# Softmax attention beside a gated MLP on one core: the order of P.V and output groups at the end, two instead of three units normalised on VectorE, and leads of TensorE's row matmuls by stretch

## The chip, the core and the metric

The kernel runs on one core of one Trainium2 chip. A core has five engines that run their own instruction streams in order and meet through semaphores: TensorE (PE; its weight loads are shown as PEld), VectorE (DVE), ScalarE (ACT), GpSimd (POOL) and SyncE (SP), which here issues all DMA transfers. TensorE writes its results into eight PSUM banks of 128 x 512 f32. The metric is device microseconds of one execution.

## What is computed

```python
def reference(A_x, A_wqkv, A_wo, B_x, B_w1, B_w3, B_w2):
    x = A_x                                   # 1 x 2048 x 512, bf16
    xn = _layernorm(x, axis=-1)
    return x + _A_ref(xn, A_wqkv, A_wo) + _B_ref(xn, B_w1, B_w3, B_w2)

def _A_ref(x, wqkv, wo):                      # 32 heads of 16
    ...
    scores = jnp.einsum("bhqd,bhkd->bhqk", q, k) * (Dh ** -0.5)
    p = _softmax(scores, axis=-1)
    o = jnp.einsum("bhqk,bhkd->bhqd", p, v)
    return o.transpose(0, 2, 1, 3).reshape(B, S, D) @ wo

def _B_ref(x, w1, w3, w2):                    # F = 1792
    h = _silu(x @ w1) * (x @ w3)
    return h @ w2
```

The layer norm has no parameters. The scores, 32 heads x 2048 x 2048, are far the largest part: each is computed twice here, once for the row maximum and once for the exponential.

## The kernel before, in words

**Units.** The work of the attention is cut into 81 units, numbered 0 to 80: four heads (a group g, eight of them) by 256 queries, or by 128 queries at the start and in the last eight groups. The last group's four units are 77 to 80. Each unit goes through these steps:

1. *Row matmuls and maxima.* TensorE computes scores with the queries on the partitions, two matmuls of 512 keys for two heads into two banks (line 1047, "P1" in the code, banks 0 and 1 or 2 and 3 by turns). VectorE reduces the 128 x 1024 scores to 128 x 2 partial maxima (line 1089). There are 1024 such pairs of matmuls and 1024 such reductions. A pair waits for the reduction before the last, which frees its banks.
2. *Final maximum.* Partial maxima become a negated row maximum, on VectorE in the first and last units (L1226), on GpSimd in the others. It is split into two bf16 numbers in Z (L1174, L1176).
3. *Opening of a unit.* The two rows of Z are put beside the queries in QT, so that the second score matmul subtracts the maximum by itself. Near the start and in the last units a TensorE tile does this (identity matmuls on QT and Z, in the helper at L593) and ScalarE evacuates it into QT (L808).
4. *Scores again and exponential.* TensorE computes scores with the keys on the partitions (L1313, a score group fills one of banks 4 to 7, after the last maximum any bank), ScalarE takes the exponential into PT, one bank at a time (L1326) or two at once (L1356). A unit of 128 queries has 16 such groups.
5. *P.V.* TensorE multiplies PT by V, which has a column of ones for the sum (L579, 16 key tiles of four matmuls each).
6. *Normalisation.* Ordinary way: ScalarE evacuates to U (L1421), SP moves the sums to Lc (L1442), GpSimd inverts them (L1446), SP writes them to DRAM and reads them back spread over the partitions (L1451, L1455), GpSimd multiplies into `onorm` (L1466; the buffers wk_on and on_b). Fast way, for the last NFPV units (`FAST_PV`): TensorE repeats the sum over 32 rows with matmuls on `ones_t`, VectorE inverts (L1411) and multiplies (L1413) straight from PSUM.

**Other work.** TensorE also runs projections, the MLP (its evacuations at L849, L851, L855), and output tiles. The last four output tiles, 12 to 15, are cut in two: an earlier part with x and the MLP, kept in SBUF, and OUTB, eight matmuls of `onorm` by `wo` (`wo,wk_on` at L593). The eighth needs group 7, that is unit 77 for tile 12 and so on to unit 80 for tile 15. VectorE adds the two parts into osb (L960) and SP stores them (L899).

**What sets the order.** All engines' streams are written out before the kernel runs, by a planner inside `_build` that follows each engine's free time with a cost for each operation and picks the next one. For TensorE `pick_pe` chooses between the next pair for a maximum (`p1_cand`), the next score group (`p2_cand`) and other matmuls (`col_cand`, or a filling matmul on xnT and ident from `fill_cand`). Other matmuls run as long as the row matmuls are not due: pairs for a maximum are due `A_LEAD` us before VectorE runs out of work, score groups `ROW_LEAD` before ScalarE does (`RELAX` later when the units behind are not ready). `COUPLE` lets a row matmul start with the one before; `KEEP` holds score groups off the rows that the next pair needs; `PAIR_WAIT` and `COVER` decide when ScalarE takes two banks at once; `URG_WAIT`, `HORIZON` and `LOAD_RATE` decide when TensorE is filled up; `MATE` prefers neighbouring banks; `PV_LEFT` tells when a unit's P.V may take a bank. These stand in `K`. In `p1_cand`, after every 32nd pair:

```python
p1_n[0] += 1
if p1_n[0] % STRETCH == 0:
    K.at(LEADS.get(p1_n[0] // STRETCH, {}))
```

`K.at` puts all values back to their base and then sets those of the stretch's entry. Entry n is read after pair 32 n, so entry 0 is never read. `LEADS` is empty in the kernel before.

In `col_cand` the active tiles are looked at in a fixed rank, and the one whose next matmul can start first is taken:

```python
st = P.pe_start(t.mode, None, P.ready("pe", reads, writes))
if best is None or st < best[0] - 1e-6:
    best = (st, t, reads, writes, g[2])
```

`red_n` counts the maxima that were put out, `NP1` is 1024; at `red_n[0] >= NP1` the last maximum is done.

## Time and profile before

| | |
|---|---|
| median of 3 runs | 1198.83 us (1197.3 to 1199.32) |
| the profiled execution | 1196.87 us, of which the span from first to last instruction is 1195.2 |
| TensorE, busy | 1122.1 us (94%) |
| VectorE, busy | 1178.8 us (99%) |
| ScalarE, busy | 1171.8 us (98%) |
| GpSimd, busy | 466.5 us (39%) |
| first maximum starts, last opening of a unit | 14.75 us, 1178.73 us |
| granted TensorE clock, mean | 0.999 |

How to read it: a busy time is the union of an engine's instructions. The mean of one instruction in a group is its own length; where instructions overlap in a pipeline (exponentials have a mean of 643 ns), a row of several in the timeline gives the pitch, its length divided by the count. In timelines the columns are start and length in us, engine, line, operation, output and input, the count that was merged, and in brackets the idle time ahead and what ended it. In a table by stretches of time each engine has its busy time and, in brackets, its instructions; the last three columns are the granted clock, the share of the DMA engines and GB/s.

### The profile page before, as it was taken

The page shows a single profiled execution, that of the slowest core. Times are in us where ns is not written, and L with a number is a line of the kernel's source. Part 1 is how long each engine was busy: PE and PEld are TensorE (multiplying, and loading weights), DVE is VectorE, ACT ScalarE, POOL GpSimd, SP SyncE. Part 2 cuts the span into 40 slices and gives each one's busy share as a digit, 9 for nine tenths or more (in the row PEclk, how much of TensorE's full clock was granted, in tenths as well). Part 3 has the DMA queues.
Part 4 walks back from the last instruction along what each step waited for, and adds up shares of the span by engine and source line. Part 5 has one row for each costly group of instructions (what it writes and reads, how often), then busy time and mean ns, then how long its engine had stood idle before and what let it go on. Part 6 is the DMA issues. An engine that isn't in the chain of part 4 may idle for free.

```text
span 1195.2 us, 34930 instructions
## 1 busy us (share of the span) xinstructions
PE 1122.1 (94%) x14546; PEld 495.0 (41%) x14711; DVE 1178.8 (99%) x1082; ACT 1171.8 (98%) x2324; POOL 466.5 (39%) x940
## 2 busy tenths in 40 slices
PE   8999999999999999999999999999989999899998
PEld 3433333343333343333443333333333555555454
DVE  8999999999999999999999999999999999999995
ACT  7899999999999999999999999999999999999997
POOL 7253645324654323656234345522133333324220
PEclk9999999999999999999999999999999999999999
DMA  6422222012212101221011121010000111000000
GB/s 194 116 51 77 59 66 68 15 40 61 52 33 60 40 19 37 57 51 42 26 37 41 48 55 44 25 28 20 22 16 19 46 33 27 20 16 16 10 12 22
DMA packets 131978, 51.54 MB, mean 43 GB/s; under 512 B 99940, under 2 KB 131820, under 8 KB 131820
## 3 DMA queue, kind: packets, MB, share of 16 engines
q1 hardware_dynamic: 131820, 49.31, 16.6%
q8 instruction: 115, 1.88, 0.7%
q14 instruction: 43, 0.35, 0.1%
HBM read 38.86 MB, written 6.74 MB: 38 GB/s over the span
## 4 chain that ended last, share of the span: by engine, by line
ACT 47%; PE 36%; DVE 14%; issue 2%; DMA 0%; POOL 0%; SPq 0%; POOLq 0%
ACT PT L1326 35%; DVE part L1089 13%; PE ps L593 12%; PE ps L1313 11%; PE ps L579 8%; ACT PT L1356 5%; PE ps L1047 5%; ACT th L849 2%; ACT zg L851 1%; ACT U L1421 1%; ACT ub L855 1%; ACT kq L755 1%; DMA PT<-in_A_x_dram 0%; PE ps L677 0%; ACT QT L808 0%
## 5 line engine op out<-in xcount | busy, mean ns | idle before, releaser
L1089 DVE TENSOR_REDUCE part<-ps 128x2 f32<-128x1024 f32 x1024 | 1160.1, 1210 | 0.8 <-PE ps L1047 0.7
L1326 ACT ACTIVATE PT<-ps 128x512 bf16<-128x512 f32 x1826 | 958.8, 643 | 2.1 <-PE ps L1313 0.9
L1313 PE MATMUL ps<-QT,KT 32*128 32x256 bf16 (+1 forms) x5184 | 564.9, 249 | 10.1 <-ACT PT L1356 5.8
L1047 PE MATMUL ps<-KT,QT 32*128 32x512 bf16 x2048 | 400.0, 384 | 5.7 <-DVE part L1089 2.1
L1313 PEld LDWEIGHTS ps<-QT,KT 32*128 32x128 bf16 x5184 | 234.0, 92 | 235.8 <-issue 96.9
L1446 POOL TENSOR_TENSOR Rc<-Lc,mone 128x8 f32<-128x8 f32 (+1 forms) x78 | 109.0, 1397 | 202.5 <-DMA Lc<-U 202.3
L579 PE MATMUL ps<-PT,Vaug 128*17 128x256 bf16 (+1 forms) x5184 | 180.5, 252 | 4.5 <-ACT zg L851 1.5
L593 PE MATMUL ps<-xnT,ident 128*128 128x512 bf16 (+1 forms) x540 | 158.4, 345 | 20.3 <-ACT PT L1356 4.6
L593 PE MATMUL ps<-xnT,w 128*128 128x512 bf16 (+1 forms) x553 | 145.9, 330 | 13.8 <-ACT zg L851 5.3
L1047 PEld LDWEIGHTS ps<-KT,QT 32*128 32x128 bf16 x2048 | 97.9, 91 | 114.3 <-issue 51.5
L579 PEld LDWEIGHTS ps<-PT,Vaug 128*17 128x17 bf16 x5184 | 90.6, 89 | 79.2 <-issue 56.1
L1356 ACT ACTIVATE PT<-ps 128x1024 bf16<-128x1024 f32 x111 | 114.8, 1062 | 1.2 <-PE ps L1313 1.0
L1197 POOL TENSOR_TENSOR mx<-part 128x16 f32<-128x16 f32 (+1 forms) x70 | 14.6, 208 | 223.0 <-DVE part L1089 222.9
L836 POOL TENSOR_TENSOR a<-zg,ub 128x512 f32<-128x512 bf16 x56 | 64.5, 1152 | 68.4 <-ACT ub L855 68.4
L593 PEld LDWEIGHTS ps<-xnT,ident 128*128 128x128 bf16 x617 | 46.5, 96 | 86.5 <-ACT PT L1326 43.4
L593 PEld LDWEIGHTS ps<-xnT,w 128*128 128x128 bf16 x588 | 44.8, 97 | 83.4 <-issue 49.0
L593 PE MATMUL ps<-w,PT 128*128 128x512 bf16 (+1 forms) x268 | 70.1, 332 | 3.3 <-ACT U L1421 1.6
L838 POOL TENSOR_TENSOR PT<-a,t 128x512 bf16<-128x512 f32 x56 | 70.9, 1266 | 2.9
L1466 POOL TENSOR_TENSOR wk_on<-U,R 128x128 bf16<-128x128 f32 (+1 forms) x45 | 24.8, 551 | 66.3 <-DMA R<-rd 66.3
L1466 POOL TENSOR_TENSOR on_b<-U,R 128x256 bf16<-128x256 f32 (+1 forms) x33 | 23.4, 709 | 51.9 <-DMA R<-rd 51.7
L851 ACT ACTIVATE zg<-ps 128x512 bf16<-128x512 f32 x56 | 37.3, 667 | 0.0
L855 ACT ACTIVATE ub<-ps 128x512 bf16<-128x512 f32 x56 | 37.2, 664 | 0.0
(90 smaller groups left out, 552.6 us busy)
## 6 DMA issues: line engine op xcount, KB each, us to landing
w<-in_B_w_dram SPq DMA_DIRECT2D x112, 128.0 KB
R<-rd SPq DMA_DIRECT2D x47, 128.0 KB
QT<-qd SPq DMA_DIRECT2D x31, 128.0 KB
KT<-kd SPq DMA_DIRECT2D x28, 128.0 KB
xr<-in_A_x_dram SPq DMA_DIRECT2D x16, 128.0 KB
out_dram<-osb SPq DMA_DIRECT2D x16, 128.0 KB
R<-rd SPq DMA_DIRECT2D x31, 64.0 KB
qd<-kq SPq DMA_DIRECT2D x15, 128.0 KB
```

The lines of the kernel that those rows point to most:

```text
L579: ins = e.matmul(bank(bk)[32 * i:32 * i + m, c0 + a:c0 + b], make_lhsT(i), rhs if (a, b) == (0, ncols) else rhs[:, a:b], start=start, stop ...
L593: return e.matmul(bank(bk)[0:rows, c0 + a:c0 + b], lhsT, rhs if (a, b) == (0, ncols) else rhs[:, a:b], start=start, stop=stop, **kw)
L836: q.append(_Item(lambda e: e.tensor_tensor(a32[:, :], zg[:, ss, :], ub[:, ss, :], ALU.mult), [("zg", ss), ("ub", ss)], [("a32",)], 1.1, 1.25))
L838: q.append(_Item(lambda e: e.tensor_tensor(hT[:, hslot(idx), :], a32[:, :], t1[:, :], ALU.mult), [("a32",), ("t1",)], [("hT", hslot(idx))] ...
L851: _Item(lambda e: e.activation(zg[:, ss, :], bank(bk), ACTF.Identity, scale=0.5), [("ps", bk)], [("zg", ss)], _c_act(512), cb=part_done, n ...
L855: return [_Item(lambda e: e.activation(ub[:, ss, :], bank(bk), ACTF.Identity), [("ps", bk)], [("ub", ss)], _c_act(512), cb=part_done)]
L1047: ins = e.matmul(bank(2 * sl + i), QT[32 * j:32 * j + 32, qs, q * 128:(q + 1) * 128], KT[32 * j:32 * j + 32, g, c_ * 512:(c_ + 1) * 512], ...
L1089: redq.append(_Item(lambda e: e.tensor_reduce(dst, pair_ap.rearrange("p (a b) -> p a b", b=512), AX.X, ALU.max), writes, [("part", par, qt ...
L1313: ins = e.matmul(bank(b)[:, i * nq:(i + 1) * nq], KT[32 * j:32 * j + 32, g, (k0 + i) * 128:(k0 + i + 1) * 128], QT[32 * j:32 * j + 32, qs, ...
L1326: expq.append(_Item(lambda e: e.activation(PT[:, sl, :], bank(b), ACTF.Exp, scale=SCALE), [("ps", b)], [pt_key(sl)], _c_act(512), cb=cb, e ...
L1356: return _Item(lambda e: e.activation(PT[:, s0:s1 + 1:s1 - s0, :], ps8[:, b0:b1 + 1:b1 - b0, :], ACTF.Exp, scale=SCALE), [("ps", b0), ("ps ...
L1446: poolq["nrm"].append(_Item(lambda e: e.tensor_tensor(Rc[:, pp, 0:nl], Lc[:, pp, 0:nl], mone[:, 0:nl], ALU.pow), [("Lc", pp), ("mone",)], ...
```

## The change

Three things: a term in the choice between the active tiles, the number of units that are normalised the fast way, and a table of leads.

```diff
-    LEADS = {}
+    LEADS = {
+        0: {'PAIR_WAIT': 0.108, 'URG_WAIT': 0.098},
+        1: {'ROW_LEAD': 0.465, 'COUPLE': 0.167, 'A_LEAD': 0.651},
+        2: {'PV_LEFT': 6, 'RELAX': 0.065, 'A_LEAD': 0.649},
...
+        12: {'URG_WAIT': 0.098, 'COVER': 0.917, 'LOAD_RATE': 4870},
+        15: {'MATE': 0.117, 'A_LEAD': 0.571, 'PV_LEFT': 6, 'URG_WAIT': 0.059},
...
+        27: {'PV_LEFT_S': 2, 'ROW_LEAD': 0.43, 'PAIR_WAIT': 0.185, 'LOAD_RATE': 4785},
+        30: {'PAIR_WAIT': 0.018, 'KEEP': 0.007, 'LOAD_RATE': 4588, 'RELAX': 0.09, 'A_LEAD': 0.684},
+    }
...
+    TAIL_PV = 0.25
...
-    NFPV = 3
+    NFPV = 2
...
-                if best is None or st < best[0] - 1e-6:
-                    best = (st, t, reads, writes, g[2])
+                key = st - (TAIL_PV if red_n[0] >= NP1 and t.name.startswith("PV") else 0.0)
+                if best is None or key < best[5] - 1e-6:
+                    best = (st, t, reads, writes, g[2], key)
```

Entries 4, 17, 20 and 21 are left out above; they set `RELAX` and `KEEP`, `COVER` and `ROW_LEAD`, `HORIZON`, `ROW_LEAD`. The base values are `ROW_LEAD` 0.45, `A_LEAD` 0.7, `RELAX` 0.06, `KEEP` 0.1, `PAIR_WAIT` 0.05, `COVER` 0.6, `URG_WAIT` 0.12, `HORIZON` 0.3, `LOAD_RATE` 5000, `PV_LEFT` 6, `PV_LEFT_S` 2, `MATE` 0, `COUPLE` 0.12. With the term, P.V is taken ahead of an output matmul that could start up to 0.25 us sooner, from the last maximum on. The added lines move every later line of the code: L1089 becomes L1102, L1313 becomes L1326, L1326 becomes L1339 and so on, 13 or 14 on.

**VectorE around the last maximum.** The rows are the engine's instructions in order, from the final maximum of unit 79 (the first row); negm is the negated maximum, wk_on the buffer of normalised outputs. Before:

```order
L1226 TENSOR_REDUCE negm<-part 128x4
L1089 TENSOR_REDUCE part<-ps 128x2 x6
L1411 RECIPROCAL R<-ps 128x128
L1413 TENSOR_TENSOR wk_on<-ps,R 128x128
L1089 TENSOR_REDUCE part<-ps 128x2
L1226 TENSOR_REDUCE negm<-part 128x4
L1174 TENSOR_SCALAR Z<-negm 128x4
L1176 TENSOR_TENSOR Z<-negm,Z 128x4
```

And now:

```order
L1239 TENSOR_REDUCE negm<-part 128x4
L1102 TENSOR_REDUCE part<-ps 128x2 x7
L1239 TENSOR_REDUCE negm<-part 128x4
L1187 TENSOR_SCALAR Z<-negm 128x4
L1189 TENSOR_TENSOR Z<-negm,Z 128x4
```

The reciprocal and the multiply of unit 78 are gone from between the last two maxima. (The first row in both is the final maximum that comes one reduction after its unit's end.)

**ScalarE from the opening of unit 80 (L808, now L821) to its last instruction.** A shape 128x2x512 is a pair of banks. Before:

```order
L808 ACTIVATE QT<-ps 128x128
L1326 ACTIVATE PT<-ps 128x512 x2
L1356 ACTIVATE PT<-ps 128x2x512
L1326 ACTIVATE PT<-ps 128x512 x2
L1356 ACTIVATE PT<-ps 128x2x512
L1326 ACTIVATE PT<-ps 128x512
L1356 ACTIVATE PT<-ps 128x2x512
L1326 ACTIVATE PT<-ps 128x512 x2
L1356 ACTIVATE PT<-ps 128x2x512
L1326 ACTIVATE PT<-ps 128x512 x2
```

And now:

```order
L821 ACTIVATE QT<-ps 128x128
L1339 ACTIVATE PT<-ps 128x512 x3
L1369 ACTIVATE PT<-ps 128x2x512
L1339 ACTIVATE PT<-ps 128x512
L1369 ACTIVATE PT<-ps 128x2x512
L1339 ACTIVATE PT<-ps 128x512 x2
L1369 ACTIVATE PT<-ps 128x2x512
L1339 ACTIVATE PT<-ps 128x512
L1369 ACTIVATE PT<-ps 128x2x512
L1339 ACTIVATE PT<-ps 128x512
L1369 ACTIVATE PT<-ps 128x2x512
```

Behind the opening stood nine single exponentials and four pairs, 17 groups; now eight and five, 18 groups. Ahead of it, between the openings of units 79 and 80, stood 15 singles and a pair; now 14 singles, a pair, and the evacuation of U for unit 78, five exponentials behind the opening of unit 79.

**TensorE at the end.** Rows with Vaug and ones_t are P.V of unit 80, one key tile each pair of rows; rows with wo are output matmuls. Before:

```order
L593 MATMUL ps<-wo,wk_on 128x512 x9
L579 MATMUL ps<-PT,Vaug 17x128 x4
L579 MATMUL ps<-PT,ones_t 32x128 x4
L579 MATMUL ps<-PT,Vaug 17x128 x4
L579 MATMUL ps<-PT,ones_t 32x128 x4
L579 MATMUL ps<-PT,Vaug 17x128 x4
L579 MATMUL ps<-PT,ones_t 32x128 x4
L579 MATMUL ps<-PT,Vaug 17x128 x4
L579 MATMUL ps<-PT,ones_t 32x128 x4
L593 MATMUL ps<-wo,wk_on 128x512
```

And now:

```order
L592 MATMUL ps<-PT,Vaug 17x128 x4
L592 MATMUL ps<-PT,ones_t 32x128 x4
L592 MATMUL ps<-PT,Vaug 17x128 x4
L592 MATMUL ps<-PT,ones_t 32x128 x4
L606 MATMUL ps<-wo,wk_on 128x512 x10
```

Nine output matmuls stood ahead of the last four key tiles; now all 16 key tiles of unit 80 stand ahead of the last ten output matmuls. The eighth matmul of tile 13 now waits for GpSimd (the product of unit 78) and has six score groups behind it. The order on TensorE is the same up to the 32nd pair for a maximum; over the whole kernel the filling matmuls (`xnT,ident`) fall from 417 of 512 and 200 of 256 columns to 400 and 203.

More of the change, by code (lines that the diff above doesn't have):

```diff
@@ L278, in _build @@
     P_PACED = False
-    LEADS = {}
+    LEADS = {
+        0: {'PAIR_WAIT': 0.108, 'URG_WAIT': 0.098},
+        1: {'ROW_LEAD': 0.465, 'COUPLE': 0.167, 'A_LEAD': 0.651},
+        2: {'PV_LEFT': 6, 'RELAX': 0.065, 'A_LEAD': 0.649},
+        4: {'RELAX': 0.07, 'KEEP': 0.034},
+        12: {'URG_WAIT': 0.098, 'COVER': 0.917, 'LOAD_RATE': 4870},
+        15: {'MATE': 0.117, 'A_LEAD': 0.571, 'PV_LEFT': 6, 'URG_WAIT': 0.059},
+        17: {'COVER': 0.481, 'ROW_LEAD': 0.411},
+        20: {'HORIZON': 0.174},
+        21: {'ROW_LEAD': 0.462},
+        27: {'PV_LEFT_S': 2, 'ROW_LEAD': 0.43, 'PAIR_WAIT': 0.185, 'LOAD_RATE': 4785},
+        30: {'PAIR_WAIT': 0.018, 'KEEP': 0.007, 'LOAD_RATE': 4588, 'RELAX': 0.09, 'A_LEAD': 0.684},
+    }
     TOL = 0.0
@@ L1601, in col_cand @@
                 st = P.pe_start(t.mode, None, P.ready("pe", reads, writes))
-                if best is None or st < best[0] - 1e-6:
-                    best = (st, t, reads, writes, g[2])
+                key = st - (TAIL_PV if red_n[0] >= NP1 and t.name.startswith("PV") else 0.0)
+                if best is None or key < best[5] - 1e-6:
+                    best = (st, t, reads, writes, g[2], key)
             if best is None:
                 return None
-            st, t, reads, writes, dur = best
+            st, t, reads, writes, dur, _ = best
             fn = best[1].groups[0][0](best[1].bank)
```

## The prediction

> **What bounds the kernel now.** I read the page first: the busy shares, then the two groups that fill the span.
>
> ```profile
> span 1195.2 us, 34930 instructions
> PE 1122.1 (94%) x14546; PEld 495.0 (41%) x14711; DVE 1178.8 (99%) x1082; ACT 1171.8 (98%) x2324; POOL 466.5 (39%) x940
> L1089 DVE TENSOR_REDUCE part<-ps 128x2 f32<-128x1024 f32 x1024 | 1160.1, 1210 | 0.8 <-PE ps L1047 0.7
> L1326 ACT ACTIVATE PT<-ps 128x512 bf16<-128x512 f32 x1826 | 958.8, 643 | 2.1 <-PE ps L1313 0.9
> ```
>
> VectorE's 1024 row maxima are 1160.1 us of work (1.133 us each) with 0.8 us of idle time ahead of them. ScalarE is as full. Neither engine gets less of this work, so the middle of the kernel can give back only stalls. Of VectorE's two waits in it, the timeline shows both:
>
> ```profile
> 117.65 1.23 DVE L1089 TENSOR_REDUCE part<-ps 128x2 f32<-128x1024 f32 x1 [0.22 <-PE ps L1047]
> 574.06 0.39 PE L1047 MATMUL ps<-KT,QT 32*128 32x512 bf16 x4
> 574.49 1.23 DVE L1089 TENSOR_REDUCE part<-ps 128x2 f32<-128x1024 f32 x1 [0.50 <-PE ps L1047]
> ```
>
> Together 0.72 us: the row matmuls came late. What is left is the tail. VectorE's timeline there:
>
> ```profile
> 1167.80 6.87 DVE L1089 TENSOR_REDUCE part<-ps 128x2 f32<-128x1024 f32 x6
> 1174.59 0.94 DVE L1411 RECIPROCAL R<-ps 128x128 f32<-128x128 f32 x1
> 1175.57 0.29 DVE L1413 TENSOR_TENSOR wk_on<-ps,R 128x128 bf16<-128x128 f32 x1
> 1175.78 1.22 DVE L1089 TENSOR_REDUCE part<-ps 128x2 f32<-128x1024 f32 x1
> 1177.44 0.18 DVE L1176 TENSOR_TENSOR Z<-negm,Z 128x4 bf16<-128x4 f32 x1
> ```
>
> Unit 78's fast normalisation sits ahead of the very last row maximum and holds it for 1175.78 - 1174.59 = 1.19 us; unit 80, the last, cannot begin before it. ScalarE, and the start of TensorE's next row matmuls:
>
> ```profile
> 1169.60 0.27 ACT L808 ACTIVATE QT<-ps 128x128 bf16<-128x128 f32 x1
> 1169.76 8.04 ACT L1326 ACTIVATE PT<-ps 128x512 bf16<-128x512 f32 x15
> 1177.82 1.02 ACT L1356 ACTIVATE PT<-ps 128x1024 bf16<-128x1024 f32 x1
> 1178.73 0.27 ACT L808 ACTIVATE QT<-ps 128x128 bf16<-128x128 f32 x1
> 1179.20 0.60 PE L1313 MATMUL ps<-QT,KT 32*128 32x128 bf16 x12
> 1186.68 1.09 ACT L1326 ACTIVATE PT<-ps 128x512 bf16<-128x512 f32 x2
> ```
>
> L808 is the evacuation that opens a unit: unit 79 at 1169.60, unit 80 at 1178.73. The last exponential ends at 1186.68 + 1.09 = 1187.77. After it, TensorE and then VectorE:
>
> ```profile
> 1187.59 0.23 PE L579 MATMUL ps<-PT,ones_t 128*32 128x128 bf16 x4
> 1187.98 1.89 PE L593 MATMUL ps<-wo,wk_on 128*128 128x512 bf16 x8 [0.16 <-issue]
> 1189.80 0.23 PE L579 MATMUL ps<-PT,Vaug 128*17 128x128 bf16 x4
> 1190.19 0.23 PE L579 MATMUL ps<-PT,ones_t 128*32 128x128 bf16 x4
> 1191.81 0.39 PE L593 MATMUL ps<-wo,wk_on 128*128 128x512 bf16 x1 [1.39 <-DVE wk_on L1413]
> ...
> 1188.39 0.69 DVE L960 TENSOR_TENSOR osb<-ps,th 128x512 bf16<-128x512 f32 x1 [3.39 <-PE ps L593]
> 1190.47 0.96 DVE L1411 RECIPROCAL R<-ps 128x128 f32<-128x128 f32 x1 [1.39 <-PE ps L579]
> 1191.46 0.29 DVE L1413 TENSOR_TENSOR wk_on<-ps,R 128x128 bf16<-128x128 f32 x1
> 1192.24 0.69 DVE L960 TENSOR_TENSOR osb<-ps,zg 128x512 bf16<-128x512 f32 x1 [0.48 <-PE ps L593]
> ```
>
> The last four key tiles of unit 80's P.V could start right after the last exponential, but stand behind output groups until 1189.80. Then comes a strict chain: reciprocal, multiply, one matmul, one add, one store, ending at 1195.20. From the last exponential to the end: 1195.20 - 1187.77 = 7.43 us.
>
> **The change, part by part.** *P.V ahead of output groups.* In the new order all of unit 80's P.V stands ahead of the last ten output matmuls. Count from the last exponential's end. TensorE sees it 0.20 later (evacuation over at 1179.00, row matmuls at 1179.20). The last four key tiles take 0.39 from first to last start (1189.80 to 1190.19), the next output matmul starts 0.39 after that (1187.59 to 1187.98): 0.98. Output matmuls follow each other at (1.89 - 0.39) / 7 = 0.214, so the tenth starts at 0.98 + 9 x 0.214 = 2.91. VectorE: reciprocal at 0.20 + 0.67 = 0.87 (1189.80 to 1190.47), multiply over 0.99 + 0.29 later, at 2.15. That is ahead of 2.91, so the reciprocal chain now hides behind the output matmuls, and these set the end (by order there are nine output matmuls in the old row of eight; at nine the pitch is 0.19 and the gain 0.2 us more). The add follows 0.43 after the tenth matmul's start (1191.81 to 1192.24) and takes 0.69; 1192.93 to 1195.20 is 2.27 for the store. Sum 6.30 against 7.43: **-1.13 us**. Bounds: if the outputs cost nothing, the multiply sets the end, (2.15 + 0.06) against (1191.81 - 1187.77 = 4.04): -1.83. If the last store must wait out the one before it, which is now issued about 0.5 us ahead and was 3.85 us ahead (1188.39 to 1192.24), nothing is won: 0. I take -1.13, nearest to the rows; they show issue times, and nothing that queues.
>
> *Two fast units instead of three.* Reciprocal and multiply of unit 78 leave VectorE: the last maximum ends 1.19 earlier. In return ScalarE gets one evacuation of U, TensorE loses 64 small ones-matmuls, and SP and GpSimd get one more normalisation. Those two queues are idle here: one earlier unit's chain shows it.
>
> ```profile
> 1163.49 0.30 ACT L1421 ACTIVATE U<-ps 128x128 f32<-128x128 f32 x1
> 1163.82 0.54 SPq L1442 DMA_DIRECT2D Lc<-U  x1
> 1165.65 1.01 POOL L1446 TENSOR_TENSOR Rc<-Lc,mone 128x4 f32<-128x4 f32 x1 [1.58 <-DMA Lc<-U]
> 1168.09 0.56 SPq L1455 DMA_DIRECT2D R<-rd  x1
> 1171.24 0.46 POOL L1466 TENSOR_TENSOR wk_on<-U,R 128x128 bf16<-128x128 f32 x1 [2.77 <-DMA R<-rd]
> ```
>
> 8.21 us from U's evacuation to the product (1163.49 to 1171.70). Who waits for it now is TensorE: the eighth matmul of output tile 13 waits for GpSimd, with score matmuls queued behind it. U's evacuation stands five exponentials behind unit 79's opening, at about 1172.3, so the product is there at 1180.5. The waiting matmul stands behind 11 of the 17 score groups left, which with four banks ahead means that some 7.5 exponentials are done: 1177.7 (the opening done 1.19 earlier) + 7.5 x 0.49 = 1181.4. It is hidden with 0.9 us to spare; without that cover ScalarE would starve for what is missing.
>
> How much of the 1.19 us arrives at the end depends on ScalarE. What one exponential costs:
>
> ```profile
> 223.12 7.87 ACT PT L1326 x16
> 847.91 2.76 ACT PT L1356 x3
> ```
>
> 0.49 single, 0.92 a pair of two. Behind unit 80's opening the old order has nine singles and four pairs, the new one eight and five: one exponential more, +0.43. So -1.19 + 0.43 = **-0.76 us**, if ScalarE reaches the opening 1.19 earlier. Bound: from opening to opening it took 9.13 us (1169.60 to 1178.73) with 15 singles; now 14 singles and U, -0.49 + 0.30 = -0.19. If ScalarE can do no better, the last exponential moves by -0.19 + 0.43 = +0.24. Other end: -0.76. I take -0.76: the 15 singles took 8.04, which is 0.69 more than 15 x 0.49, so ScalarE was fed slowly there and has room. TensorE allows it: its work ends at 1190.42 before the final wait; 1.19 earlier, with one output matmul (0.214) and one score group (a third of 0.42 to 0.60) more, its tenth output matmul could start at 1189.6, ahead of 1187.77 - 0.76 + 2.91 = 1189.92.
>
> *Leads by stretch.* Apart from fillers, instruction counts stay; the order on TensorE moves, from the 33rd row matmul pair on (entry 0 of the table is never read). At 574.06 the old order has three score groups and 24 P.V matmuls between two pairs of row matmuls, each group waiting for ScalarE; the new one has two groups and 16 there. At 117.65 the place is re-ordered but no lighter (28 P.V matmuls and two groups). Three groups between two pairs are about as frequent as they were (208 places before, 214 now), and one of the 208 cost something. Bounds: -0.72 (both waits go, none come) to +0.72 (both stay, as many come). I take **-0.6**, the first wait and half of the second. ScalarE can follow: from maxima 832 to 992 the new order has two exponentials (0.98 us) more behind it.
>
> Sum: -1.13 - 0.76 - 0.6 = **-2.5 us**. The profiled execution took 1196.87 (span 1195.20 and 1.67 around it), so 1194.4; the median of the runs lies 1.96 above it, which gives **1196.3 us**.
>
> [...] The new order has 15.5 fewer 512-column filling matmuls on xnT and ident, and lower load targets in three stretches. The granted clock:
>
> ```profile
> 1177.00:1187.80 10.80, 10.48 (x319) 6.62 (x321) 3.15 (x7) 10.44 (x17) 0.00 (x0) 1.00 0.09 27
> 1187.80:1195.20 7.40, 2.85 (x45) 1.29 (x42) 2.63 (x4) 0.00 (x0) 0.00 (x0) 0.90 0.11 37
> ```
>
> It was 1.00 with TensorE 97% busy (10.48 of 10.80) and 0.90 in the last stretch, where it is mostly idle: 0.74 us of clock lost in 7.40. The missing fillers are 15.5 x 0.214 = 3.3 us. By the rows they cost nothing while other work is dense, and at most their own 3.3 us. I take nothing; the other end is rival (3). [...]
>
> **Rivals.** (1) *ScalarE does not follow*: the opening of unit 80 comes no earlier and the stalls stay; only -1.13 is left, 1197.7. For it: ScalarE is 98% busy. Against: the 0.69 us it was fed late. (2) *Row matmuls come late, slower*: in stretches 1, 2, 15 and 30 the lead of the maxima's row matmuls is cut by 0.049, 0.051, 0.129 and 0.016. A usual pair and the eight maxima around it:
>
> ```profile
> 1149.55 9.13 DVE L1089 TENSOR_REDUCE part<-ps 128x2 f32<-128x1024 f32 x8
> 1154.65 0.39 PE L1047 MATMUL ps<-KT,QT 32*128 32x512 bf16 x2
> ```
>
> It starts 0.55 ahead of its maximum (the sixth of the eight, at 1155.20); at 574.06 to 574.49 it was 0.43 and VectorE waited. So there is 0.12 to lose, and stretch 15 loses 0.129. If all 32 maxima of each stretch lose the whole cut, that is 7.8 us: 1204.1. It makes the kernel slower from 4.9 us on. Against: the lead is a target, and most pairs are far ahead. (3) *The clock drops where fillers are gone*: up to 3.3 us, 1199.6. Against: the row's 1.00. (4) *The product for tile 13 comes late*: 0.9 us of room and four banks (1.96 us) cover it; from 2.9 us late each further us counts. Six us late: 1199.4.
>
> **How the numbers follow.** Under 0.2% (2.4 us) a measurement of this kernel cannot tell a difference. Chances: forecast 0.48; (1) 0.31; (2) 0.14; (3) 0.03; (4) 0.04. The likeliest case's own range is -1.83 - 0.76 - 0.72 to +0.24 + 0.72, so 1195.5 to 1199.8, and runs spread 1 us around. The range reaches 1194.4 to 1200.8, leaving most of (2) out and some 0.05 below. Faster 0.48; within 0.2% 0.38, from (1), (3) and (4); slower 0.14, from (2).
>
> **What would show it.** Right: the last maximum follows the 1023rd without a gap; the last exponential ends near 1186.4 of the span; behind it P.V, then ten output matmuls in a row, the final add some 3.3 us after the exponential, with no wait for the multiply. Wrong: a wait of TensorE on GpSimd near 1181 with ScalarE idle, waits of the maxima of over 2 us in total, a granted clock under 1.00 before 1187, or a final store longer than 2.3 us. The prediction fails outright if the last maximum does not end earlier.

## The result, and the profile after

| | before | after |
|---|---|---|
| median of the runs, us (range) | 1198.83 (1197.3 to 1199.84, 5 runs) | 1193.87 (1193.64 to 1193.98, 5 runs) |
| profiled execution, us; its span | 1196.87; 1195.2 | 1193.98; 1192.0 |
| last row maximum starts | 1175.78 | 1173.90 |
| unit 80 opens | 1178.73 | 1176.91 |
| last exponential ends | 1187.78 | 1186.09 |
| from there to the end | 7.42 | 5.91 |

The ratio on record is 0.9966, with an interval from 0.9954 to 0.9978 (the two medians alone give 0.9959): faster, by more than the 0.2% that can be told. The profiled span is 3.2 us shorter where the sum of the prediction said 2.5. The median is 4.96 us lower, and the last part of the experiments is about the difference between 4.96 and 3.2. Times up to the end of the span, here and below, go by spans that the page gives to 0.1 us.

The page of the changed kernel, busy shares and the two groups that fill the span:

```profile
span 1192.0 us, 34780 instructions
PE 1115.8 (94%) x14463; PEld 490.7 (41%) x14628; DVE 1177.6 (99%) x1080; ACT 1170.0 (98%) x2328; POOL 469.7 (39%) x942
L1102 DVE TENSOR_REDUCE part<-ps 128x2 f32<-128x1024 f32 x1024 | 1160.0, 1212 | 0.1
L1339 ACT ACTIVATE PT<-ps 128x512 bf16<-128x512 f32 x1832 | 960.0, 642 | 2.7 <-PE ps L1326 1.5
```

The maxima cost what they did (1160.0 us of work); the 0.8 us of idle time ahead of them has become 0.1. VectorE's timeline of the changed kernel shows the place of the old 0.50 us wait, and then the tail:

```profile
565.75 14.79 DVE L1102 TENSOR_REDUCE part<-ps 128x2 f32<-128x1024 f32 x13
...
1167.12 8.00 DVE L1102 TENSOR_REDUCE part<-ps 128x2 f32<-128x1024 f32 x7
1175.15 0.17 DVE L1239 TENSOR_REDUCE negm<-part 128x4 f32<-128x16 f32 x1
1186.82 0.96 DVE L1424 RECIPROCAL R<-ps 128x128 f32<-128x128 f32 x1 [3.57 <-PE ps L592]
1187.81 0.29 DVE L1426 TENSOR_TENSOR wk_on<-ps,R 128x128 bf16<-128x128 f32 x1
1189.07 0.69 DVE L973 TENSOR_TENSOR osb<-ps,zg 128x512 bf16<-128x512 f32 x1 [0.37 <-PE ps L606]
```

Thirteen maxima in a row pass 574 without a bracket; the last seven maxima stand in one row, with no reciprocal ahead of the very last; and the last add waits for TensorE's output matmul, no longer for a matmul that itself waits for the multiply. ScalarE, TensorE (matmuls, and the weight loads of the output matmuls), SP and GpSimd of the changed kernel in the tail:

```profile
1168.42 0.27 ACT L821 ACTIVATE QT<-ps 128x128 bf16<-128x128 f32 x1
1171.08 0.28 ACT L1434 ACTIVATE U<-ps 128x128 f32<-128x128 f32 x1
1175.68 0.55 SPq L1468 DMA_DIRECT2D R<-rd  x1
1176.91 0.27 ACT L821 ACTIVATE QT<-ps 128x128 bf16<-128x128 f32 x1
1179.03 0.46 POOL L1479 TENSOR_TENSOR wk_on<-U,R 128x128 bf16<-128x128 f32 x1 [4.79 <-DMA R<-rd]
1185.02 1.07 ACT L1369 ACTIVATE PT<-ps 128x1024 bf16<-128x1024 f32 x1
1186.14 0.23 PE L592 MATMUL ps<-PT,Vaug 128*17 128x128 bf16 x4
1186.54 0.23 PE L592 MATMUL ps<-PT,ones_t 128*32 128x128 bf16 x4
1186.70 1.84 PEld L606 LDWEIGHTS ps<-wo,wk_on 128*128 128x128 bf16 x10
1186.93 2.10 PE L606 MATMUL ps<-wo,wk_on 128*128 128x512 bf16 x9 [0.16 <-issue]
```

The last exponential ends at 1185.02 + 1.07 = 1186.09; P.V goes on 0.05 later, and the output matmuls follow it in one row. Ten weight loads stand ahead of nine recorded matmuls. The nine start 0.216 apart, from 1186.93 to 1188.65, and the add starts 0.42 behind the last of them, as it started 0.43 behind the lone matmul before. So the tenth record, which the trace lacks, is that of the first, near 1186.71. The row of eight in the kernel before lacks its first one too, since nine weight loads stand there:

```profile
1187.74 1.63 PEld L593 LDWEIGHTS ps<-wo,wk_on 128*128 128x128 bf16 x9
```

The product of unit 78 is ready at 1179.49, 8.41 us after U's evacuation.

The difference of the two profiled executions can be added up along one chain. From the first maximum to the last: 0.74 less waiting in the middle and 1.19 less between the last two maxima, which with a start 0.05 later makes -1.88. Unit 80 opens 2.96 behind the last maximum before and 3.00 after. From the opening to the last exponential's end: 9.04 and 9.18. From there to the end: 7.42 and 5.91. Together -1.88 + 0.04 + 0.14 - 1.51 = -3.2.

### The profile page after: what moved, and what is told of

It reads as the page before. It is cut to its first block, busy times and chain, and to the rows that moved or that the text cites. A ratio compares the mean times of both kernels' runs of the same rounds, so it can differ in the third digit from the quotient of the medians.

```text
span 1192.0 us, 34780 instructions
## 1 busy us (share of the span) xinstructions
PE 1115.8 (94%) x14463; PEld 490.7 (41%) x14628; DVE 1177.6 (99%) x1080; ACT 1170.0 (98%) x2328; POOL 469.7 (39%) x942
## 4 chain that ended last, share of the span: by engine, by line
ACT 51%; PE 23%; DVE 20%; issue 3%; POOL 2%; DMA 1%; POOLq 0%
ACT PT L1339 39%; DVE part L1102 20%; PE ps L606 7%; PE ps L1326 7%; PE ps L592 6%; ACT PT L1369 5%; PE ps L1060 3%; ACT th L862 2%; ACT zg L864 1%; ACT U L1434 1%; ACT ub L868 1%; ACT kq L768 1%; POOL a L849 1%; ACT osb L928 0%; DMA R<-rd 0%
## 5 line engine op out<-in xcount | busy, mean ns | idle before, releaser
L1102 DVE TENSOR_REDUCE part<-ps 128x2 f32<-128x1024 f32 x1024 | 1160.0, 1212 | 0.1
L1339 ACT ACTIVATE PT<-ps 128x512 bf16<-128x512 f32 x1832 | 960.0, 642 | 2.7 <-PE ps L1326 1.5
L1326 PE MATMUL ps<-QT,KT 32*128 32x256 bf16 (+1 forms) x5184 | 563.2, 249 | 9.4 <-ACT PT L1369 4.5
L1326 PEld LDWEIGHTS ps<-QT,KT 32*128 32x128 bf16 x5184 | 234.4, 92 | 235.7 <-issue 93.6
L592 PE MATMUL ps<-PT,Vaug 128*17 128x256 bf16 (+1 forms) x5184 | 182.9, 252 | 6.2 <-ACT PT L1369 3.0
L606 PE MATMUL ps<-xnT,ident 128*128 128x512 bf16 (+1 forms) x525 | 153.0, 344 | 20.7 <-ACT PT L1369 7.3
L1369 ACT ACTIVATE PT<-ps 128x1024 bf16<-128x1024 f32 x108 | 112.0, 1062 | 0.8 <-PE ps L1326 0.5
L606 PE MATMUL ps<-w,PT 128*128 128x256 bf16 (+1 forms) x287 | 71.6, 322 | 3.0 <-issue 1.8
L846 POOL TENSOR_SCALAR t<-th 128x512 f32<-128x512 bf16 x56 | 34.8, 621 | 7.9 <-ACT th L862 5.7
```

Source lines behind the costliest of these rows:

```text
L592: ins = e.matmul(bank(bk)[32 * i:32 * i + m, c0 + a:c0 + b], make_lhsT(i), rhs if (a, b) == (0, ncols) else rhs[:, a:b], start=start, stop ...
L606: return e.matmul(bank(bk)[0:rows, c0 + a:c0 + b], lhsT, rhs if (a, b) == (0, ncols) else rhs[:, a:b], start=start, stop=stop, **kw)
L1102: redq.append(_Item(lambda e: e.tensor_reduce(dst, pair_ap.rearrange("p (a b) -> p a b", b=512), AX.X, ALU.max), writes, [("part", par, qt ...
L1326: ins = e.matmul(bank(b)[:, i * nq:(i + 1) * nq], KT[32 * j:32 * j + 32, g, (k0 + i) * 128:(k0 + i + 1) * 128], QT[32 * j:32 * j + 32, qs, ...
L1339: expq.append(_Item(lambda e: e.activation(PT[:, sl, :], bank(b), ACTF.Exp, scale=SCALE), [("ps", b)], [pt_key(sl)], _c_act(512), cb=cb, e ...
L1369: return _Item(lambda e: e.activation(PT[:, s0:s1 + 1:s1 - s0, :], ps8[:, b0:b1 + 1:b1 - b0, :], ACTF.Exp, scale=SCALE), [("ps", b0), ("ps ...
```

## The experiments

Line numbers differ by some units from kernel to kernel, since each edit moves the lines. "At full clock" below means runs whose mean granted TensorE clock is .999 or 1.0.

### The three parts apart

**P.V ahead of the outputs alone** (`LEADS = {}`, three fast units):

```
+    TAIL_PV = 0.25
...
-                if best is None or st < best[0] - 1e-6:
-                    best = (st, t, reads, writes, g[2])
+                key = st - (TAIL_PV if red_n[0] >= NP1 and t.name.startswith("PV") else 0.0)
+                if best is None or key < best[5] - 1e-6:
+                    best = (st, t, reads, writes, g[2], key)
```

> Only the P.V term of 0.25 us, with three fast units and an empty table; the order is that of before up to the last maximum. Theory of three terms (output groups -1.5 us, two fast units -1.0, leads -0.7 by the two profiled spans): the last exponential ends where it did, 1187.8 +- 0.3, the end comes 5.9 to 6.3 us after it, span 1193.7 to 1194.2. Rival, the spread (runs of before differ by 2.5 us and those of the change by 0.3, so one part removes a stall that comes and goes): if the tail's order is what steadies the kernel, the runs lie within 0.5 us of each other and the median falls by over 2.5 us; if not, they still spread by 2 us and the median falls by 1.0 to 1.5.

Measured: 1195.58 us median of 11 runs, ratio 0.9983 (0.9974 to 0.9992); two of the eleven had a lower clock, .998 and .997 (1196.55 and 1197.44). Its profiled span is 1193.8, so -1.4. The last maximum (1175.76) and the last exponential (1187.65) are where they were; the end behind them takes 6.15. Its TensorE and VectorE there:

```profile
1187.70 0.23 PE L580 MATMUL ps<-PT,Vaug 128*17 128x128 bf16 x4
1188.10 0.23 PE L580 MATMUL ps<-PT,ones_t 128*32 128x128 bf16 x4
1188.48 2.32 PE L594 MATMUL ps<-wo,wk_on 128*128 128x512 bf16 x10 [0.16 <-issue]
...
1188.38 0.96 DVE L1412 RECIPROCAL R<-ps 128x128 f32<-128x128 f32 x1 [3.29 <-PE ps L580]
1189.37 0.29 DVE L1414 TENSOR_TENSOR wk_on<-ps,R 128x128 bf16<-128x128 f32 x1
1190.84 0.69 DVE L961 TENSOR_TENSOR osb<-ps,zg 128x512 bf16<-128x512 f32 x1 [0.58 <-PE ps L594]
```

Reciprocal and multiply end at 1189.66, ahead of the last output matmul: they are hidden, as the working had it. With eleven output matmuls behind P.V in this order (ten recorded) the add starts 3.19 behind the exponential; with ten, in the changed kernel, 2.98.

**Two fast units alone** (`LEADS = {}`, no P.V term):

```
-    NFPV = 3
+    NFPV = 2
```

> Only two fast units, no P.V term, empty table. Three terms: the last maximum starts 1.19 us earlier (1174.6), the last exponential ends 0.2 to 0.9 earlier; by its order only five output matmuls are left behind the last P.V, so the end comes 6 to 6.6 us after it: span 1193.2 to 1194.8. If two fast units gain nothing by themselves (ScalarE sets the end), the last exponential stays at 1187.8. Spread theory: runs steady within 0.5 us only if unit 78's fast normalisation was what came and went.

Measured: 1195.62 median of 11 runs, 0.9984 (0.9975 to 0.9993). Seven were at full clock (median 1195.40), four at .998 or .997 (1196.30 to 1197.88). The order shows something that the prediction had not looked at: with two fast units the planner puts all 16 key tiles of unit 80's P.V ahead of the last five output matmuls by itself, without the new term. So this edit alone shortens the end too (6.02 behind the last exponential), and the two gains cannot be added. Its profiled run is one in which the clock fell; it is used further down.

**Both, without the leads** (`TAIL_PV = 0.25`, `NFPV = 2`, `LEADS = {}`):

> The P.V term and two fast units, with an empty table: the change without its leads. Three terms: span 1192.7 to 1193.2 (0.7 above the change's 1192.0), VectorE still waits 0.7 us in the middle. Spread theory with the leads as cause: the runs spread by 2 us and the median stays 2 us or more above the change's 1193.87. If the leads do nothing: median 1194.0 and runs within 0.5 us.

Measured: 1195.14 median of 10 runs, 0.9976 (0.9967 to 0.9985), span 1193.4: 0.4 us better than the P.V term alone. All ten runs were at .999 or 1.0 and lie within 1.0 us of each other, so the expectation that they spread by 2 us without the leads failed; this counts further down. ScalarE from the opening of unit 80 to its last exponential in this kernel:

```profile
1177.61 0.28 ACT L809 ACTIVATE QT<-ps 128x128 bf16<-128x128 f32 x1
...
1185.60 1.02 ACT L1357 ACTIVATE PT<-ps 128x1024 bf16<-128x1024 f32 x1
1186.52 1.18 ACT L1327 ACTIVATE PT<-ps 128x512 bf16<-128x512 f32 x2
```

The opening comes 1.12 earlier than before (1178.73), so the last maximum's 1.15 does arrive there. But by the order 19 groups stand behind it, where before there were 17, and they take 10.09 us against 9.04. The last exponential ends at 1187.70, 0.08 earlier. Between the openings of units 79 and 80 ScalarE now takes 15 groups, where before it took 17. The time that VectorE won is work that ScalarE had not yet done.

**The leads alone** (three fast units, no P.V term, the whole table):

> Only the table of leads, three fast units, no P.V term. Three terms: VectorE's waits in the middle go (0.7 us), the last maximum starts at 1175.1, the last exponential ends near 1187.1, and since by its order 16 output matmuls stand behind the last P.V, the end comes 7.2 to 7.6 us after it: span 1194.4 to 1194.8, median -0.5 to -1. Spread theory with the leads as its cause: the runs lie within 0.5 us and the median falls by 2.5 us or more, while the three kernels with an empty table keep a spread of 2 us.

Measured: 1196.7 median of 11 runs (1196.39 to 1197.07), 0.9989 (0.998 to 0.9998). From the first maximum to the last it takes 1160.29 in place of 1161.03, 0.74 less, and the last one starts at 1175.34 although the first one starts 0.30 late. No wait of the maxima on TensorE is left in its table of waits. The order has 18 groups behind the opening of unit 80 in place of 17, and all 16 output matmuls behind P.V; the last exponential ends at 1187.90, not near 1187.1 as expected, and the span is the old 1195.2. Alone, the leads gain nothing at the end. Together with the other two parts they move the last exponential from 1187.70 to 1186.09: 0.70 because the opening comes sooner (1176.91 for 1177.61), and 0.91 because 18 groups stand behind the opening in place of 19.

### Which entries of the table

**Entries 12 to 30 alone, and entries 1 to 4 alone**, each with the other two parts:

```
-        1: {'ROW_LEAD': 0.465, 'COUPLE': 0.167, 'A_LEAD': 0.651},
-        2: {'PV_LEFT': 6, 'RELAX': 0.065, 'A_LEAD': 0.649},
-        4: {'RELAX': 0.07, 'KEEP': 0.034},
```

and, in the second kernel, the other way round:

```
-        12: {'URG_WAIT': 0.098, 'COVER': 0.917, 'LOAD_RATE': 4870},
...
-        30: {'PAIR_WAIT': 0.018, 'KEEP': 0.007, 'LOAD_RATE': 4588, 'RELAX': 0.09, 'A_LEAD': 0.684},
```

> The changed kernel with only the table's entries of the stretches 12, 15, 17, 20, 21, 27 and 30; the order of TensorE is that of the kernel before up to the 409th pair of rows (about 476 us). Theory (the place near 198 us, where the clock fell to half in the run with two fast units alone, is what the entries of stretches 1, 2 and 4 re-plan): this kernel keeps the place, so some of its runs show a granted clock of .996 to .998 and lie 1 to 2.5 us above its fastest; VectorE's wait of .57 at 572.8 is gone and that of .30 at 116.2 stays. For the end there are two theories. If the entries of the last stretches give ScalarE its lead, the last exponential ends within .5 of the changed kernel's 1186.1 and the fastest run is near 1194.3. If the lead is gathered over the whole table, it ends between 1186.5 and 1187.7, and the fastest run lies near 1194.7 to 1195.2. By the order 22 groups of exponentials stand behind the last opening (18 in the changed kernel), which speaks for the second. Rival on the clock (each re-planned order has its own luck, with no one place): all runs at 1.0.

> The changed kernel with only the table's entries of the stretches 1, 2 and 4. Theory of the place near 198 us: all runs at a granted clock of 1.0, spread under .7 us. VectorE's wait at 116.2 is gone, that of .57 at 572.8 may stay (the order behind it is planned anew). The end as without the table if the last stretches' entries give ScalarE its lead: last exponential near 1187.7, time about 1194.9 to 1195.2; in between (1186.5 to 1187.5, about 1194.3) if the lead is gathered over the whole table. Rival on the clock: some runs at .997 all the same.

Measured: with the late entries 1196.15 median of 11 runs; its eight runs at full clock have a median of 1196.0, longer than with no table at all (1195.14). By the order 22 groups stand behind the last opening, and they took 11.17 us. Even its fastest run, 1195.77, lies above both times that were expected. With the early entries 1193.98 median of 7 runs, and the five at full clock have 1193.84, like the whole table. In the profiled run of each the clock fell (below), so the second was looked at once more:

> The changed kernel with only the entries of the stretches 1, 2 and 4 once more, for a profile at full clock. Its runs at 1.0 took what the changed kernel takes (1193.8), so either ScalarE has its lead from the early entries alone (last opening near 1176.9, last exponential near 1186.1), or the last maximum comes later and fewer groups are left behind it. If the run falls into the drop: 17 us of half clock from 915 again, about 6.5 us longer.

It took 1194.32. ScalarE's first and last rows of its tail:

```profile
1176.87 0.27 ACT L813 ACTIVATE QT<-ps 128x128 bf16<-128x128 f32 x1
...
1185.96 1.02 ACT L1361 ACTIVATE PT<-ps 128x1024 bf16<-128x1024 f32 x1
```

The opening stands at 1176.87, as with the whole table (1176.91), and the waits in the middle are gone as well. The last exponential ends 0.9 later (1186.98; 19 groups), but only six output matmuls are left behind P.V, and the end takes 5.51. So the entries for stretches 1, 2 and 4 carry the gain at full clock. The waits at 117.65 and 574.49 both go, though the second lies in none of these stretches: everything behind the 32nd pair is planned anew. ScalarE's lead comes neither from the late entries nor from the whole table by degrees: the late half alone makes the kernel longer, and the early half alone takes as long as the whole table, though not by the same way, with 19 groups behind the opening and a shorter end.

**One fast unit:**

```
-    NFPV = 2
+    NFPV = 1
```

> The changed kernel with only the last unit's P.V on the fast evictions (NFPV 1). The order differs from the changed kernel's only behind the 4658th row of TensorE, where the P.V of unit 78 is put behind output groups. ScalarE bounds the end, so if unit 78's eviction was what made room for the last openings, the last exponential stays at 1186.1 and the time is 1193.9 within .3; if its multiply and add now come late for the outputs, .5 to 1 us slower.

Measured: 1194.31 median of 10 runs, 0.9975 (0.9965 to 0.9984): 0.4 slower than the changed kernel. Unit 79's U is now a row of ScalarE behind the last opening:

```profile
1177.31 0.27 ACT L821 ACTIVATE QT<-ps 128x128 bf16<-128x128 f32 x1
1179.98 0.27 ACT L1434 ACTIVATE U<-ps 128x128 f32<-128x128 f32 x1
1186.23 0.59 ACT L1339 ACTIVATE PT<-ps 128x512 bf16<-128x512 f32 x1
```

The time lies between the two cases that were expected. From the opening to the last exponential's end it takes 9.51 against 9.18: the 0.27 of U stands on ScalarE's path. So beside the other two parts two fast units are better than one; three beside both was not run.

### Where the other 1.8 us of the median come from

The median fell by 4.96, the profiled span by 3.2. The runs of the kernel before are not all alike: on the chip of the first experiments, 15 of its 32 runs had a granted clock of .999 or 1.0 (median 1197.0), 11 had .996 or .997 (1198.34 to 1199.94), six .998 (1197.35 to 1198.13). The 5 runs of the changed kernel and the 11 with its leads alone all had 1.0. In the kernel with two fast units alone, the profiler caught a run at .997. Columns of this view: stretch, its length, busy time of TensorE, weight loads, VectorE, ScalarE and GpSimd, granted clock, DMA share, GB/s.

```profile
195.00:198.46 3.46, 2.92 (x34) 1.13 (x38) 3.46 (x4) 3.46 (x8) 3.23 (x5) 1.00 0.20 51
198.46:205.29 6.83, 6.50 (x86) 2.25 (x75) 5.10 (x5) 4.40 (x9) 1.83 (x7) 0.50 0.07 17
```

The kernel before, in its profiled execution, in the same stretches:

```profile
195.00:198.46 3.46, 2.92 (x35) 1.13 (x38) 3.46 (x4) 3.46 (x8) 3.25 (x5) 1.00 0.19 43
198.46:205.29 6.83, 6.50 (x106) 2.81 (x95) 6.82 (x7) 6.35 (x13) 2.19 (x8) 1.00 0.09 23
```

The order of the two is the same up to unit 78. In one the clock falls to half for 6.83 us, TensorE gets through 86 matmuls where it had done 106, and VectorE is busy for 5.10 where it had been for 6.82. From the first maximum to the last it took 1162.25, where the kernel with both tail edits, of the same order up to the last maximum, took 1159.82: 2.4 us more. The kernel with the late entries alone, whose order is that of the kernel before up to 476 us, was caught at the same place:

```profile
195.20:198.65 3.45, 2.91 (x38) 1.16 (x34) 3.45 (x4) 3.45 (x8) 3.20 (x6) 1.00 0.18 49
198.65:205.48 6.83, 6.50 (x82) 2.18 (x71) 5.21 (x5) 4.51 (x9) 1.81 (x7) 0.50 0.06 13
```

That spoke for one weak place, re-planned by the early entries. The kernel with the early entries alone refutes it: two of its 7 runs had .993 and took 1200.5 and 1201.0. The profiled one of these, and behind it the changed kernel in the same stretches:

```profile
911.60:915.00 3.40, 2.38 (x28) 0.80 (x25) 3.40 (x4) 3.40 (x6) 1.61 (x8) 1.00 0.11 39
915.00:922.00 7.00, 6.53 (x62) 2.41 (x61) 5.56 (x5) 4.27 (x8) 0.72 (x1) 0.50 0.04 7
```

```profile
911.60:915.00 3.40, 2.74 (x30) 0.99 (x28) 3.40 (x4) 3.40 (x6) 1.62 (x8) 1.00 0.12 39
915.00:922.00 7.00, 6.43 (x121) 3.38 (x119) 7.00 (x7) 7.00 (x16) 1.29 (x4) 1.00 0.11 26
```

Here the half clock lasted 17.07 us and cost some 6.5: from the first maximum to the last 1165.62, and 1159.15 in the execution of the same kernel at full clock. So there is no one place. Nor does the order alone decide. The kernel with both tail edits has the order of the kernel before to beyond 1150 us, and on the same chip the clock fell in none of its ten runs. With 11 in 32 for each run, ten in a row without a fall would be a chance of under 2%. What else decides, no run here shows.

To see what makes a place, three kernels changed the filling matmuls (`xnT,ident`), whose results nobody reads, and left the order as it is. In the kernel before, the filling matmul near 197.1 was lengthened:

```
-                P.pe(all_groups(bk, ident[:, :], xnT[:, 0, 0:256], 256),
+                fn = all_groups(bk, ident[:, :], xnT[:, 0, 0:256], 256)
+                if 196 < st < 198:
+                    one = all_groups(bk, ident[:, :], xnT[:, 0, 0:512], 512)
+                    fn = lambda e: (one(e), one(e))[1]
+                P.pe(fn,
```

> The kernel before, in which one filling matmul, that near 197.1 us, is made four times as long (two of 512 columns for one of 256); its results are read by nobody, and the order is the same. Theory (too little work on TensorE between 195 and 198.5 us lets the clock fall at 198.5): all runs at a granted clock of 1.0 or .999, time 1196.6 to 1197.2, no run above 1197.5, while the kernel before on the same chip has a third of its runs at .996 to .998 and 1198 to 1200. The row matmuls behind the filling one come .32 us later at most, so a wait of up to .3 may be added. [...]

Measured: 10 of 11 runs at full clock (median 1196.99), one at .996 (1199.39). The kernel before on the same chip had 3 of 31 at .996, so this tells nothing: on that chip the drop was too rare.

In the changed kernel, the filling matmuls between 180 and 300 us were made 16 columns wide:

```
-                P.pe(all_groups(bk, ident[:, :], xnT[:, 0, 0:512], 512),
+                n = 16 if 180 < st < 300 else 512
+                P.pe(all_groups(bk, ident[:, :], xnT[:, 0, 0:n], n),
```

and the same for those of 256 columns.

> The changed kernel, in which the 38 filling matmuls between 180 and 300 us are 16 columns wide instead of 256 or 512; their results are read by nobody, and the order is the same. Theory (TensorE's clock falls to half where too little streams through it): the clock falls between 180 and 300 us in most or all runs, by one or more stretches of about 6.83 us, each of which costs about 2.4 us as in the run with two fast units alone (VectorE waits for row matmuls at half speed): granted clock .997 or lower, 1196 us or more. Rival (light stretches are not what the clock answers to): all runs at 1.0 and 1193.9 us.

Measured: 7 of 12 runs at full clock, 1193.79 median; the other five at .998 (1194.78), .993 (1198.84, 1199.40, 1199.86) and .989 (1202.88). These falls are fewer than the "most or all" that was expected. The profiled run was one without a fall, so where the five fell is not shown. The changed kernel has the same order, and its 13 runs (5, and 8 below) were all at 1.0, but the eight were on another chip, and for the five no chip is on record. On this chip the kernel before never had less than .996. Thinner still, from 180 to 600 us:

> The changed kernel with the 119 filling matmuls between 180 and 600 us 16 columns wide (38 between 180 and 300 in the run before). [...]

Measured: 1205.88 at .984, with three falls of the clock: at 195.50 for 17.07 us, at 311.55 and at 478.80 for 10.24 us each. What VectorE lost:

```profile
DVE part L1102 <- PE ps L1326: 7.4, 13, 1.1
DVE part L1102 <- PE ps L1060: 2.3, 3, 1.3
```

Those are 9.7 us of new waits of the maxima in this kernel's table of waits (us in total, times, longest); the changed kernel has no row `part <- PE`. Its stretches around the last fall, and behind them those of the changed kernel on the same chip:

```profile
475.00:478.80 3.80, 3.69 (x30) 1.40 (x29) 3.80 (x4) 3.80 (x9) 3.33 (x7) 1.00 0.33 86
478.80:489.04 10.24, 9.88 (x102) 3.12 (x101) 7.72 (x7) 7.58 (x14) 4.31 (x7) 0.50 0.15 34
```

```profile
475.00:478.80 3.80, 3.64 (x61) 1.62 (x54) 3.80 (x5) 3.79 (x10) 0.17 (x1) 1.00 0.31 70
478.80:489.04 10.24, 9.45 (x72) 3.21 (x71) 10.24 (x10) 10.20 (x21) 6.40 (x11) 1.00 0.23 54
```

TensorE was busy for 97% of the stretch ahead of the fall (3.69 of 3.80). Busy time doesn't tell what the clock answers to. I weighed the matmuls of the 3.415 us ahead of each fall instead (half of the shortest fall, 6.83): columns streamed, times four where the trace shows a matmul of more than 32 rows and 32 columns (up to 128*128), else times one (row matmuls, 32*128, and P.V, 128*17). Length and weights are my choice, and no run shows that the clock goes by them. They give:

```
fall at    kernel            weighted columns   changed kernel, same window
198.46     two fast alone    12032              15872
198.65     late entries      12800              16128
915.04     early entries     12288              14336
195.50     thin to 600       10368              13312
311.55     thin to 600       11904              17408
478.80     thin to 600       11904              20224
```

All six falls follow windows of at most 12800 (the mean of the changed kernel is some 17300), and in the same windows the changed kernel is heavier. But it is no threshold: the kernel before shows the same 12032 ahead of 198.46 in the execution where the clock stayed. Nor are such windows rare. Counted from any start, without overlap, the profiled execution of the changed kernel passes 55 of them between 40 and 1185 us (the lightest 9984, from 1019.67), and that of the kernel before 54 (9728, from 847.28), all at full clock. So light windows stand ahead of the falls, but most of them are followed by none. Last, the changed kernel once more on a third chip, where the kernel before had 3 of 18 runs at .996 or .997:

> The changed kernel as it is, eleven runs on another chip. Theory (its order has no stretch that lets the clock fall): all runs at a granted clock of 1.0, 1193.6 to 1194.3 us, and against the runs of the kernel before that are at 1.0 a gain of 2.5 to 3.2. Rival (its few runs so far were lucky): two or three of eleven runs at .993 to .998, 1 to 5 us longer.

Measured: all 8 runs at 1.0, 1193.84 median (1193.35 to 1194.52), ratio 0.9972 (0.9962 to 0.9982). Against the runs of the kernel before at full clock there (median 1196.89 of 13) that is -3.05 us.

## Why the prediction was right, and where it was off

In the changed kernel the mechanism was the one forecast in each of the three parts, and the sum of -2.5 stands against -3.2 in the profiled spans and -3.05 in runs at full clock. Point by point:

- **P.V ahead of the outputs, -1.13.** Measured -1.51 in the changed kernel, -1.27 alone. The chain is the one worked out: multiply hidden, output matmuls set the end, final store as before (2.24 us, against 2.27). Two sizes were off. The lag from the last exponential to TensorE is 0.05 and not 0.20, which was taken from one place. And there was one step too many: the 0.39 that the prediction read from P.V to the next output matmul (1187.59 to 1187.98) reach to the first recorded one, which is the second in the order, so eight steps follow and not nine. The pitch of 0.214 was right (0.216 by the starts), and the prediction's bracket, with nine matmuls in the old row and 0.19, was wrong. Less 0.15 and less one step, 3.34 becomes 2.98, where the add does start; with eleven and nine output matmuls behind P.V (the P.V term alone, and with two fast units) it starts at 3.19 and 2.76.
- **Two fast units, -0.76.** The last maximum follows the 1023rd without a gap, and its 1.19 arrives at the opening of unit 80, which comes 2.75 to 3.07 behind the last maximum in every kernel here. The term +0.43 for one exponential more was 0.14 in the changed kernel. But without the leads it was +1.05, and the outcome of rival (1) came true, though not by its way: the opening came 1.12 earlier, but two groups more stood behind it, and nothing was gained ahead of the last exponential. The prediction costed this part by the changed kernel's order, so the sum holds; but it gave to the fast units what belongs to the fast units and the leads together. The room that it saw in ScalarE (0.69 us fed late) was not enough for the fast units alone. In the changed kernel unit 79 opens 1.18 sooner already (1168.42 for 1169.60), and ScalarE takes 8.49 from there to the opening of unit 80, for 9.13 before.
- **Leads, -0.6.** Both waits in the middle went, and 0.74 was won, near the bound of 0.72. That is all that the term named. The second effect, one group fewer behind the last opening (0.91 us), was inside the count of groups used for the part above.
- **The clock, 0.** The working said that fewer fillers cost nothing "while other work is dense", and looked at the profiled execution alone, where the clock is 1.00 up to the last stretch. That execution was one of the luckier ones. The step that failed is the last one of the sum: "the median of the runs lies 1.96 above it, which gives 1196.3 us". The 1.96 were taken for a property of the program that the change leaves alone, and by that the measured 1193.87 lies 0.5 below the range that was given (1194.4 to 1200.8). By the granted clocks of the later runs the 1.96 are the price of falls of the clock: 2.4 us and more each, in a third of the runs on one chip, a tenth on another and a sixth on a third. The clocks of the first runs of the kernel before, which gave the 1.96, are not on record but for the profiled one, so for them this is argued. The changed order had no fall in 13 runs, nor had its leads in 11 more, so its median lies at its profiled time. Whether its order is the reason stays open, since the ten runs with both tail edits had none without the leads. No profile of the kernel before caught a fall; that it falls near 198.5 is argued from two kernels with its order up to there.
- **Rival (2)**, row matmuls late from the smaller leads, did not show: no wait of the maxima on TensorE is left in the table of waits. **Rival (3)** did not come true for the changed kernel, which had no fall, though falls came with thinner fillers (in five of 12 runs, and in the one run with them thin to 600 us). That its order has fewer light windows is not shown: its profiled execution passes 55, that of the kernel before 54. **Rival (4)** did not show: the product was ready at 1179.49, ahead of the 1181.4 at which the prediction saw it needed, no wait of TensorE for it stands in the table of waits, and its chain took 8.41 against 8.21.

## What to carry to other kernels

Where two engines are full, time won on one at the end reaches the end only if the other has done its share by then: count what stands behind the last opening in the order, and not only when it opens (with both tail edits it opened 1.12 earlier with 19 groups behind it, and the last exponential ended 0.08 earlier). Edits of an order do not add up: with a planner, each part has to be costed on the order that the whole change makes. And before adding the distance from the profiled run to the median, read the granted clock of every run: if the runs differ by it, that distance is no fixed cost of the program, and the next kernel's runs may be without it or have more of it.

A row of matmuls can lack a record (here nine stood beside ten weight loads, and eight beside nine): count the weight loads beside it, and take the pitch from two starts, before a count is put into a sum.

## What was not expected of the hardware

TensorE's clock fell to half (0.50 in the rows) in the middle of the kernel, at a mean load that kept it busy for 94% of the span, in some runs of one and the same program and not in others. The six falls that were caught follow windows that are light in streamed columns, weighted as above (10368 to 12800, where the changed kernel has a mean of 17300), while busy time tells less: in the stretches shown ahead of four of them TensorE was busy for 70% to 97%. But windows of 12800 or less pass at full clock in both kernels' profiled executions (54 before, 55 after), so what brings a fall stays open. One fall costs 2.4 us for 6.83 us of half clock (1162.25 - 1159.82 from the first to the last maximum, with two fast units alone and with both tail edits), 6.5 for 17.07 (1165.62 - 1159.15, the two profiles with the early entries). With two fast units alone, VectorE's maxima waited 1.79 us for TensorE around the fall (0.44, 0.31, 0.89 and 0.15, from 199.16 to 205.96). Filling matmuls whose results nobody reads were worth their place here: with 119 of them cut to 16 columns, the kernel took 12 us longer in its one run (1205.88, against 1193.84 on the same chip).
